# Dilated window attention and a gated MLP: plain q and k of six batches come through the crossbar, in the layout of the direct batches

## The chip, the cores and the metric

The kernel runs on one core of a Trainium2 chip. The metric is the device time of one execution in microseconds (us). Three executions of the kernel before took 310.85, 311.17 and 311.59 us; their median, 311.17, is the time before. The profile was taken from an execution of its own, with a span of 309.7 us.

## The reference

Attention over 8 batches, 8 heads, 576 tokens, 64 channels. Heads 0 to 3 ("plain") see the last 32 tokens, heads 4 to 7 ("dilated") every fourth of the last 128. An MLP with a swish gate follows.

```python
scores = scale * np.matmul(q, k.transpose(0, 1, 3, 2))
rel = pos[:, None] - pos[None, :]
mask_plain = (rel >= 0) & (rel < window)                                         # window 32, heads 0-3
mask_dil = (rel >= 0) & (rel < window * dilation) & (rel % dilation == 0)         # dilation 4, heads 4-7
attn = softmax(np.where(masks, scores, -1e9))
attn_out = np.matmul(attn, v)
x = attn_out.transpose(0, 2, 1, 3).reshape(B * S, H * D)      # 4608 tokens x 512
h = x @ w_in                                                   # 512 x 2048
g = h * (1.0 / (1.0 + np.exp(-beta * h)))
return g @ w_out                                               # 2048 x 512
```

Inputs and output are fp32; the kernel computes in bf16 with fp32 sums.

## The kernel before

A plan is made while the program is built: operations with their inputs, a rank `vt` and expected durations. A list scheduler puts them on the engines and gives out the eight PSUM banks. The order on every engine is then fixed; at run time each instruction waits only for its data. While TensorE is expected to wait early in the kernel, matmuls on zeros ("filler") are put in.

The MLP goes through 9 tiles of 512 tokens. For each, 16 blocks of `w_in` (four matmuls of 512 columns each), a tanh on ScalarE and a gate on VectorE, and later 4 blocks of `w_out` (16 matmuls each). Attention runs batch by batch beside it and leaves its output transposed in `xT`, in four parts of 128 channels: parts 0 and 1 are plain heads, 2 and 3 dilated. In the first tile four blocks are cut at token 288:

```python
    def slot_h(t, fb, c0, n, vt, xdeps):
        g = Group("h")
        def mms(e):
            for kt in range(NKT):                                    # the four parts of xT
                nc.tensor.matmul(bank(g)[:, 0:n], lhsT=w_in_bf[:, kt, fb * P:(fb + 1) * P],
                                 rhs=xT[:, kt, xo:xo + n], start=(kt == 0), stop=(kt == NKT - 1))
        ...  # tanh on ScalarE, gate on VectorE
        split = SPLIT if t == 0 else 0                               # SPLIT = 4
        order = [(fb, 0, S // 2) for fb in range(split)] + [(fb, S // 2, NTOK - S // 2) for fb in range(split)] + [
            (fb, 0, NTOK) for fb in range(split, NFB)]
```

q and k come in two ways. Batches 0 to 2 (`DIRECT = 3`) are loaded with tokens on partitions, cast to bf16 on the way, and transposed by TensorE. From batch 3 on, q and k are cast into a contiguous bf16 copy in DRAM, and a DMA transpose (crossbar) brings them into SBUF with channels on partitions:

```python
    def cast(b, z, deps, vt):
        dst = scratch[b, z] = dram_pool.tile([2, S * 4 * D], BF16, name=f"s{b}_{z}")
        src = (k, q)[z][b].rearrange("(x h) s d -> x (h s d)", x=2)
        return load("POOL", (dst[:].rearrange("x (a e) -> (x a) e", e=1024), src.rearrange("x (a e) -> (x a) e", e=1024)), ...)

    def crossbar(b, z, h0, deps, vt):
        flat = scratch[b, z][h0 // 4]
        if h0:                                                       # dilated heads
            dst = (dk, dq)[z][b % 2][:].rearrange("p r h t -> p r (h t)")
            src = flat.rearrange("(a e) -> a e", e=C * D)
        else:                                                        # plain heads: even and odd tokens in two halves of the partitions
            dst = raw[:, z].rearrange("p h m -> p (h m)").unsqueeze(1)
            src = flat.rearrange("(a e) -> a e", e=P)
        return plan.op([("SP", 1300)], lambda e: nc.sync.dma_start_transpose(out=dst, in_=src), ...)
```

For the plain heads of these batches, even and odd tokens are then spread by copies: k into `kz`, whose other rows stay zero, q into `qd`. So there are two forms of plain score, one in halves of the array and one over all 128 rows:

```python
            for e_ in range(2):
                def spread(e, e_=e_):                                # k: 2 copies a batch; q: 4 more
                    rows = slice(64 * e_, 64 * e_ + 64)
                    dst = kz[rows, :, WIN:].rearrange("p h (m e) -> p h m e", e=2)[:, :, :, e_]
                    copy(e, dst, raw[rows, 0])
            ...
            if b < DIRECT:                                           # two heads, one in each half of the rows
                ...
                            nc.tensor.matmul(
                                bank(gs[h])[:, a * QT:(a + 1) * QT], lhsT=kT[x][rows, i * QT:i * QT + P],
                                rhs=qT[rows, x, i * QT:(i + 1) * QT], start=b >= ADDED, stop=b >= ADDED or a == 2)
                continue
            g = Group("s")
            ...                                                      # all 128 rows, one head after another
                        nc.tensor.matmul(
                            sc[:, a, h2 * QT:h2 * QT + QT],
                            lhsT=kz[:, 2 * x + h2, i * QT:i * QT + P],
                            rhs=qd[:, 2 * x + h2, :, i * QT // 2:(i + 1) * QT // 2], start=True, stop=True)
```

A score is followed by an exponential on ScalarE, a mask multiply on GpSimd or VectorE, six value matmuls and a normalisation. Dilated heads have a main part and a tail of the last 16 tokens of each of the four residues (`T`, `U`). Batches 0 and 1 go into `xT` by TensorE; from batch 2 on the rows are stored to DRAM (plain rows in two stores by parity from batch 3, the tail in four) and come back through the crossbar. The last block of the output is made of two halves, the second evacuated by two engines and stored by two queues.

Of the kernel before, what the change touches and what calls it, by code (L numbers as in the profile page):

```python
# [22 lines left out]
class Op:  # L23
    def __init__(self, engs, fn, deps, vt, acquire, group, dma, lat):
        self.engs, self.fn, self.vt, self.acquire = engs, fn, vt, acquire
        self.deps = [d for d in deps if d is not None]
        self.dma, self.lat, self.group = dma, lat, group
        self.end = self.ready = None
        self.waits = 0
        self.next = []  # L30
        for g in group if isinstance(group, list) else [] if group is None else [group]:
            g.users.append(self)


class Plan:
# [3 lines left out]
    CAPS = {"h": 3, "o": 2, "z": 4, "a": 8, "s": 5}  # L39
# [6 lines left out]
    def op(self, engs, fn, deps=(), vt=0.0, acquire=None, group=None, dma=0, lat=None):  # L46
        acquire = acquire if acquire is None or isinstance(acquire, list) else [acquire]
        o = Op(engs, fn, deps, vt, acquire, group or acquire, dma, lat)
        self.ops.append(o)
        return o  # L50

    def run(self, filler=None, filler_until=0.0):
# [13 lines left out]
        ends = []  # L66

# [19 lines left out]
        while n_left:  # L87
# [25 lines left out]
            if filler is not None and s <= filler_until and free["PE"] + 300 < s:  # L113
# [5 lines left out]
                free["PE"] = now + 225  # L119
                continue  # L120
# [6 lines left out]
            o.fn(e)  # L127
            free[e] = s + d
# [28 lines left out]
FIRST = "KD0 QD0 KD1 QD1 KP0 QP0 KP1 QP1 S2 S3 T S00 S10 V20 V21 V30 V31 U V00 V10 X2 X3 X00 X10 S01 S11 V01 V11 X01 X11"  # L157
LATER = "S2 S3 T V20 V21 V30 V31 U S00 S10 S01 S11 X2 X3 V00 V10 X00 X10 S02 S12 V01 V11 X01 X11"
# [3 lines left out]
def kernel(  # L162
# [34 lines left out]
    DIRECT = 3  # L197
    ADDED = 1
    BY_DMA = 2
    SPLIT = 4  # L200
# [16 lines left out]
    def copy(e, out, in_):  # L217
# [10 lines left out]
    mask_e = {n: const([P, 2, 2, 2, QT // 2], BF16, f"maske_{n}") for n in ("FP", "PP")}  # L228
# [14 lines left out]
    ptt = const([P, 2, 288], BF16, "ptt")  # L243
    ptt_own = ptt[0:2 * KTL][:, :, 0:256].rearrange(
        "p c (h s) -> p c h s", h=4)[:, :, :, 0:2 * UT]
# [9 lines left out]
    raw = const([P, 2, 4, S // 2], BF16, "raw")  # L255
    vd16 = raw[:].rearrange("p z h m -> p (z h m)")[:, 0:1024].rearrange("p (h T d) -> p h T d", h=4, T=C)
    vd16_of = [vd16] * DIRECT + [st[b % 2][:, 0:1024].rearrange(
        "p (h T d) -> p h T d", h=4, T=C) for b in range(DIRECT, B)]
    kT = [const([P, WIN + S], BF16, f"kT{x}") for x in range(2)]
    kz = const([P, 4, WIN + S], BF16, "kz")  # L260
    qd = const([P, 4, 2, S // 2], BF16, "qd")
    qT = qd[:].rearrange("p (x f) e m -> p x (f e m)", x=2)[:, :, 0:S]
# [27 lines left out]
    def t_fill1(e):  # L290
        for x in range(2):
            nc.vector.memset(kT[x][:, 0:WIN], 0.0)
# [61 lines left out]
    def t_late(e):  # L354
        band(mask_d[:], [[0, 4]], [(1, P)], 0, WIN - 1, 1.0, 0.0)
        for n in ("PP", "FP"):
            band(mask_e[n][:].rearrange("p a b e m -> p (a b) e m"), [[0, 4]], [(1, 2), (2, QT // 2)],
                 WIN, -1, 1.0, 0.0)
            band(mask_n[n][:].rearrange("p a b n -> p (a b) n"), [[0, 4]], [(1, QT)], WIN, -1, 1.0, 0.0)
        nc.gpsimd.memset(mask_e["FP"][0:WIN, 0], 0.0)  # L360
        nc.gpsimd.memset(mask_n["FP"][0:WIN, 0], 0.0)
        nc.gpsimd.memset(kz[:], 0.0)  # L362
    late_fill = plan.op([("POOL", 11500)], t_late, vt=-.3)


# [15 lines left out]
    def plain_v(b, p0, c0):  # L381
        return bass.AP(tensor=v.tensor, offset=v[b, 0].offset + (p0 - WIN) * D + c0 * QT * D,
                       ap=[[D, (P if not p0 else P - WIN) if not c0 else WIN], [QT * D, 4 * NI - c0], [1, D]])

    def direct_vp(b, deps, vt):
        if b:
            return [load("POOL", (vp[b % 2][:, :, 0:D], plain_v(b, 0, 0)), deps, vt, 768, .27, 1450,
                         1100 if b < DIRECT else 4000)]
        return [load("POOL", (vp[0][WIN:P, :, 0:D], plain_v(0, WIN, 0)), deps, vt, 576, .25),
                load("POOL", (vp[0][0:WIN, 1:, 0:D], plain_v(0, 0, 1)), deps, vt, 184, .25)]  # L390

    def direct_vd(b, deps, vt, tdeps=()):
        src = v[b, 4:8].rearrange("h (t T) d -> t h (T d)", T=C)[0:P]
        out = [load("POOL", (vd16_of[b].rearrange("p h T d -> p h (T d)"), src), deps, vt, 512, .35)]
        for c in range(2):
            src = bass.AP(tensor=v.tensor, offset=v[b, 4].offset + ((P - WIN) * C + c) * D,
                          ap=[[2 * D, 2 * KTL], [S * D, 4], [1, D]])
            out.append(load("POOL", (vt_[b % 2][:, c, :, 0:D], src), list(tdeps), vt + (.15 if b == 0 else .02 if b < DIRECT else 0) + .001 + .001 * c, 96, .2))
# [4 lines left out]
    def cast(b, z, deps, vt):  # L403
        dst = scratch[b, z] = dram_pool.tile([2, S * 4 * D], BF16, name=f"s{b}_{z}")
        src = (k, q)[z][b].rearrange("(x h) s d -> x (h s d)", x=2)
        return load("POOL", (dst[:].rearrange("x (a e) -> (x a) e", e=1024),
                             src.rearrange("x (a e) -> (x a) e", e=1024)), deps, vt, 1152, .38)

    def crossbar(b, z, h0, deps, vt):
        flat = scratch[b, z][h0 // 4]  # L410
        if h0:
            dst = (dk, dq)[z][b % 2][:].rearrange("p r h t -> p r (h t)")
            src = flat.rearrange("(a e) -> a e", e=C * D)
        else:
            dst = raw[:, z].rearrange("p h m -> p (h m)").unsqueeze(1)
            src = flat.rearrange("(a e) -> a e", e=P)
# [31 lines left out]
    xcopy = {}  # L448

    def back_dma(b, j, vt_of, vdone):  # L450

        rows = dram_pool.tile([S // 2, HD], BF16, name=f"x{b}_{j}")
        plain = rows[:, 0:HD // 2].rearrange("(i m e) c -> e m i c", e=2, m=QT // 2)
        out = []
        if b < DIRECT:
            out.append(plan.op(
                [("SP", 500)], lambda e: nc.sync.dma_start(
                    out=rows[:, 0:HD // 2].rearrange("(i m) c -> m i c", m=QT),
                    in_=xsp[j][:].rearrange("p a x h d -> p a (x h d)")),
                [vdone[0, j], vdone[1, j]], vt_of[f"X1{j}"], dma=1200, lat=2000))  # L460
        for e_ in range(2 if b >= DIRECT else 0):
            out.append(plan.op(
                [("SP", 500)], lambda e, e_=e_: nc.sync.dma_start(
                    out=plain[e_], in_=xsp[j][e_ * QT // 2:(e_ + 1) * QT // 2].rearrange("p a x h d -> p a (x h d)")),
                [vdone[0, j], vdone[1, j]], vt_of[f"X1{j}"], dma=600, lat=2000))
# [7 lines left out]
        if j:  # L473
            for c in range(C):
                dil.append(plan.op(
                    [("SP", 500)], lambda e, c=c: nc.sync.dma_start(
                        out=right[t1 - t0:, c], in_=xdt[(c % 2 * 2 + c // 2) * UT:(c % 2 * 2 + c // 2 + 1) * UT].rearrange("p x h d -> p (x h d)")),
                    [vdone["U"]], vt_of["X11"], dma=150, lat=2000))
# [13 lines left out]
        for x in range(4):  # L492
            xcopy[b, x, j] = o

    def attention(b, ld, names, vts):
# [4 lines left out]
        if b < DIRECT:  # L500
            for n in [x for x in names if x[0] in "KQ"]:
# [8 lines left out]
                def evac(e, g=g, z=z, kind=kind, i=i):  # L510
                    tp = bank(g, BF16)[:, 0:S]
                    if kind == "P":
                        dst = qT[:, i] if z else kT[i][:, WIN:]
# [4 lines left out]
                key = (("kT", "qT")[z], i) if kind == "P" else (("dk", "dq")[z], kv, i)  # L518
                steps[n] = [plan.op([dve(S), act(S)], evac, [tr, fill1] + war(key), vt, group=g)]
                wrote(key)  # L520
        else:
            vt = vt_of["zPRE"]
            ready = {"D": [ld["x", 0, 4], ld["x", 1, 4]]}
            ops = []
            for e_ in range(2):
                def spread(e, e_=e_):
                    rows = slice(64 * e_, 64 * e_ + 64)
                    dst = kz[rows, :, WIN:].rearrange("p h (m e) -> p h m e", e=2)[:, :, :, e_]
                    copy(e, dst, raw[rows, 0])
                o = plan.op([("POOL", 1200), ("DVE", 1400)], spread, [ld["x", 0, 0], late_fill] + war("kz"), vt)  # L530
                used(("raw", 0), o)
                ops.append(o)
            wrote("kz")
# [468 lines left out]
```

The softmax here doesn't subtract the row's maximum and nothing guards it: scores larger than these inputs give would overflow.

## Time and profile before

| what | value |
|---|---|
| time, median of three | 311.17 us |
| span of the profiled execution | 309.7 us |
| granted TensorE clock | 0.998 |
| matmuls of w_in and w_out, 512 columns | 576 and 571 recorded |
| plain scores over all rows | 120, of 96 columns |
| transposes of q and k on TensorE | 72 of 96 columns, 216 of 64 |
| DMA, software queue (casts, loads) | 19.66 MB, 42336 packets |
| DMA, hardware queue (crossbars, stores) | 22.37 MB, 51052 packets |

In the profile PE is TensorE, DVE is VectorE, ACT is ScalarE, POOL is GpSimd and SP is SyncE. A line of a timeline gives the start and length of a run of equal instructions in us, the engine, the line of the kernel, what is written from what, and, in brackets, how long the engine stood idle before and what it waited for. TensorE overlaps its matmuls, so the difference of two starts tells what one costs, and not its own length. A line of the list of DMA issues ends with the size and the median time from issue to landing.

### The profile page before, as it was taken

The page shows a single profiled execution, that of the slowest core. Times are in us where ns is not written, and L with a number is a line of the kernel's source. Part 1 is how long each engine was busy: PE and PEld are TensorE (multiplying, and loading weights), DVE is VectorE, ACT ScalarE, POOL GpSimd, SP SyncE. Part 2 cuts the span into 40 slices and gives each one's busy share as a digit, 9 for nine tenths or more (in the row PEclk, how much of TensorE's full clock was granted, in tenths as well). Part 3 has the DMA queues.
Part 4 walks back from the last instruction along what each step waited for, and adds up shares of the span by engine and source line. Part 5 has one row for each costly group of instructions (what it writes and reads, how often), then busy time and mean ns, then how long its engine had stood idle before and what let it go on. Part 6 is the DMA issues. An engine that isn't in the chain of part 4 may idle for free.

```text
span 309.7 us, 6029 instructions
## 1 busy us (share of the span) xinstructions
PE 297.0 (96%) x2270; PEld 153.6 (50%) x2307; DVE 199.1 (64%) x421; ACT 171.3 (55%) x302; POOL 108.6 (35%) x150
## 2 busy tenths in 40 slices
PE   7899999999999999999999999999999999999994
PEld 5565546454454445444455454445544444444452
DVE  4687868888958777775896878677853443434300
ACT  2668845866448445753775547555754544554311
POOL 8989754537170146414823651154000000000000
PEclk9999999999999999999999999999999999999999
DMA  6999999999689982999999759997024100001112
GB/s 100 168 210 207 206 187 208 230 155 174 155 163 178 191 151 83 180 160 181 188 206 181 197 117 177 129 224 163 18 64 112 44 34 34 36 34 60 42 70 69
DMA packets 93561, 42.48 MB, mean 137 GB/s; under 512 B 71052, under 2 KB 88220, under 8 KB 93212
## 3 DMA queue, kind: packets, MB, share of 16 engines
q0 software_dynamic: 42336, 19.66, 50.3%
q1 hardware_dynamic: 51052, 22.37, 35.0%
q8 instruction: 18, 0.29, 0.4%
q14 instruction: 11, 0.09, 0.1%
q10 hardware_dynamic: 144, 0.07, 0.1%
HBM read 39.32 MB, written 18.87 MB: 188 GB/s over the span
## 4 chain that ended last, share of the span: by engine, by line
PE 82%; POOL 6%; DMA 6%; DVE 2%; issue 2%; ACT 0%; POOLq 0%; ACTq 0%; DVEq 0%
PE bank L856 38%; PE bank L824 35%; DMA raw<-in_v_dram 3%; DMA vp<-in_v_dram 3%; PE bank L703 2%; PE bank L755 2%; POOL st L368 1%; PE bank L740 1%; PE bank L644 1%; PE bank L725 1%; POOL kz L362 1%; DVE qt L218 1%; DVE g L836 1%; PE bank L434 0%; PE bank L618 0%
## 5 line engine op out<-in xcount | busy, mean ns | idle before, releaser
L831 ACT ACTIVATE tnh<-bank,beta_half 128x512 bf16<-128x512 f32 (+2 forms) x148 | 100.1, 677 | 81.8 <-PE bank L824 73.6
L836 DVE SCALAR_TENSOR_TENSOR g<-tnh,bank 128x512 bf16<-128x512 bf16 (+2 forms) x148 | 98.7, 670 | 69.2 <-ACT tnh L831 68.1
L824 PE MATMUL bank<-xT,w_in_bf 128*128 128x512 bf16 (+2 forms) x576 | 139.8, 373 | 1.3 <-DVE xT L218 0.3
L856 PE MATMUL bank<-w_out_bf,g 128*128 128x512 bf16 (+1 forms) x571 | 137.7, 373 | 1.8 <-DVE g L836 0.5
L856 PEld LDWEIGHTS <-g 128*128 128x128 bf16 x592 | 55.4, 98 | 58.6 <-issue 0.8
L824 PEld LDWEIGHTS <-w_in_bf 128*128 128x128 bf16 x592 | 55.1, 98 | 58.2 <-issue 0.8
L873 ACT ACTIVATE osb<-bank 128x512 f32<-128x512 f32 (+2 forms) x36 | 21.0, 582 | 28.4 <-PE bank L856 23.5
L586 ACT ACTIVATE pt<-bank 128x384 bf16<-128x384 f32 (+1 forms) x54 | 22.0, 455 | 6.4 <-PE bank L703 3.5
L586 ACT ACTIVATE ptd<-bank 128x512 bf16<-128x512 f32 x32 | 17.0, 601 | 10.3 <-PE bank L644 10.3
L605 DVE TENSOR_TENSOR xsp<-bank,rcp 96x384 bf16<-96x384 f32 x32 | 17.7, 554 | 1.1
L604 DVE RECIPROCAL rcp<-bank 128x4 f32<-128x4 f32 (+2 forms) x72 | 12.8, 177 | 5.5 <-PE bank L755 2.8
L218 POOL COPY kz<-raw 64x1152 bf16<-64x1152 bf16 x6 | 9.4, 1566 | 18.4 <-DMA raw<-s 18.3
L218 POOL COPY vd<-st 128x1024 bf16<-128x1024 bf16 x4 | 4.1, 1037 | 30.9 <-DMA st<-in_v_dram 30.9
L590 DVE TENSOR_TENSOR ptd<-ptd,mask_d 128x512 bf16<-128x512 bf16 x24 | 13.0, 575 | 2.8 <-ACT ptd L586 2.5
L605 DVE TENSOR_TENSOR xdm<-bank,rcp 128x256 bf16<-128x256 f32 x32 | 13.6, 424 | 1.1
L590 POOL TENSOR_TENSOR pt<-pt,maske_FP 128x384 bf16<-128x384 bf16 x7 | 6.3, 912 | 20.4 <-ACT pt L586 12.4
L368 POOL DMA_DIRECT2D vp<-in_v_dram x9 | 12.0, 1338 | 2.6 <-DMA vp<-in_v_dram 2.6
L755 PEld LDWEIGHTS <-pt 128*128 128x128 bf16 x192 | 9.2, 97 | 6.5 <-DVE pt L590 0.6
L755 PE MATMUL bank<-vp,pt 128*128 128x65 bf16 x192 | 10.6, 193 | 0.9 <-DVE pt L590 0.5
L368 POOL DMA_DIRECT2D vt<-in_v_dram x16 | 11.0, 694 | 0.0
L875 DVE TENSOR_SCALAR osb<-bank 128x512 f32<-128x512 f32 (+1 forms) x2 | 1.0, 486 | 13.7 <-ACT osb L873 13.7
L218 DVE COPY qd<-raw 64x1152 bf16<-64x1152 bf16 x14 | 8.9, 634 | 0.9 <-DMA raw<-s 0.8
(125 smaller groups left out, 223.4 us busy)
## 6 DMA issues: line engine op xcount, KB each, us to landing
out_dram<-osb SPq DMA_DIRECT2D x35, 256.0 KB, 2.0
s<-in_k_dram POOLq DMA_DIRECT2D x5, 576.0 KB, 7.6
s<-in_q_dram POOLq DMA_DIRECT2D x5, 576.0 KB, 10.2
vp<-in_v_dram POOLq DMA_DIRECT2D x7, 384.0 KB, 14.8
w_out_bf<-in_moe_w_out_dram POOLq DMA_DIRECT2D x2, 1024.0 KB, 16.3
st<-in_k_dram POOLq DMA_DIRECT2D x6, 288.0 KB, 13.3
st<-in_q_dram POOLq DMA_DIRECT2D x6, 288.0 KB, 13.5
x<-xsp SPq DMA_DIRECT2D x20, 72.0 KB, 2.3
```

The source lines that it names most:

```text
L218: (nc.scalar.copy if e == "ACT" else E[e].tensor_copy)(out=out, in_=in_)
L368: {"POOL": nc.gpsimd, "SP": nc.sync}[queue].dma_start(out=out, in_=in_)
L586: nc.scalar.activation(out=w(), in_=sc(), func=ACT.Exp, scale=SCALE)
L590: E[e].tensor_tensor(out=w(), in0=w(), in1=m(), op=ALU.mult)
L604: nc.vector.reciprocal(out=r, in_=p[..., D])
L605: nc.vector.tensor_tensor(out=dst, in0=p[..., 0:D], in1=r.unsqueeze(len(p.shape) - 1).to_broadcast(list(p.shape[:-1]) + [D]), op=ALU.mult)
L755: nc.tensor.matmul(pv[:, a, h2, :], lhsT=pt[x][:, (3 * j + a) * 2 + h2], rhs=vp[kv][:, (2 * x + h2) * NI + 3 * j + a, 0:D + 1], start=True ...
L824: nc.tensor.matmul(bank(g)[:, 0:n], lhsT=w_in_bf[:, kt, fb * P:(fb + 1) * P], rhs=xT[:, kt, xo:xo + n], start=(kt == 0), stop=(kt == NKT - 1))
L831: nc.scalar.activation(out=th[:, 0:n], in_=bank(g)[:, 0:n], func=ACT.Tanh, scale=beta_half[:, fb:fb + 1])
L836: nc.vector.scalar_tensor_tensor(out=g_t[t % 2][:, fb, c0:c0 + n], in0=th[:, 0:n], scalar=1.0, in1=bank(g)[:, 0:n], op0=ALU.add, op1=ALU.mult)
L856: nc.tensor.matmul(bank(g)[:, lo:hi], lhsT=g_t[t % 2][:, fb, tb * P:(tb + 1) * P], rhs=w_out_bf[:, fb, lo:hi], start=(fb == 0), stop=(fb = ...
L873: nc.scalar.mul(out=ob[:, cols], in_=bank(g)[:, cols], mul=0.5)
```

## The change

Its purpose is one layout of plain q and k for all batches. The plain heads are cast into token rows (all four heads of a token side by side), so that the crossbar brings them straight into the layout of the direct batches, now double-buffered. `raw`, `kz`, `qd` and the copies into them go, and so does the second form of score. Only batches 0 and 1 stay direct. Stores of attention rows become fewer: plain rows in one store, the tail in one. In the first tile, four blocks of `w_in` are computed apart: the sum over the dilated parts of `xT` first, the plain ones later in the same bank. The tail of batches 0 and 1 gets its own transposes (`Y2`, `Y3`) and can come later. The v load of batch 0 comes in three pieces by head, its tail load is ranked later, masks are made one by one, and the scheduler is told of a cost of 95 ns for a change between half and full rows. The last output block is made in pieces of 256, 128 and 128 columns.

```diff
-    CAPS = {"h": 3, "o": 2, "z": 4, "a": 8, "s": 5}
+    CAPS = {"h": 3, "p": 4, "o": 2, "z": 4, "a": 8, "s": 5}
+    SWITCH = 95
...
-LATER = "S2 S3 T V20 V21 V30 V31 U S00 S10 S01 S11 X2 X3 V00 V10 X00 X10 S02 S12 V01 V11 X01 X11"
+LATER = "S2 S3 T V20 V21 V30 V31 U S00 S10 X2 X3 V00 V10 X00 X10 S01 S11 V01 V11 X01 X11"
...
-    DIRECT = 3
+    DIRECT = 2
...
-    SPLIT = 4
+    APART = 4
...
-    raw = const([P, 2, 4, S // 2], BF16, "raw")
-    kT = [const([P, WIN + S], BF16, f"kT{x}") for x in range(2)]
-    kz = const([P, 4, WIN + S], BF16, "kz")
-    qd = const([P, 4, 2, S // 2], BF16, "qd")
+    kT = [const([P, 2, WIN + S], BF16, f"kT{i}") for i in range(2)]
+    qT = [const([P, 2, S], BF16, f"qT{i}") for i in range(2)]
...
-        return [load("POOL", (vp[0][WIN:P, :, 0:D], plain_v(0, WIN, 0)), deps, vt, 576, .25),
-                load("POOL", (vp[0][0:WIN, 1:, 0:D], plain_v(0, 0, 1)), deps, vt, 184, .25)]
+        half = 2 * NI
+        return [load("POOL", (vp[0][WIN:P, 0:half, 0:D], plain_v(0, WIN, 0)[:, 0:half]), deps, vt, 288, .25),
+                load("POOL", (vp[0][0:WIN, 1:half, 0:D], plain_v(0, 0, 1)[:, 0:half - 1]), deps, vt, 92, .25),
+                load("POOL", (vp[0][:, half:, 0:D], plain_v(0, 0, half)), deps, vt, 384, .27)]
...
+    def cast(b, z, h0, deps, vt):
+        dst = scratch[b, z, h0] = dram_pool.tile([S * 4 * D], BF16, name=f"s{b}_{z}_{h0}")
+        src = (k, q)[z][b, h0:h0 + 4]
+        if h0:
+            args = (dst[:].rearrange("(a e) -> a e", e=1024), src.rearrange("h s d -> (h s d)").rearrange("(a e) -> a e", e=1024))
+        else:
+            args = (dst[:].rearrange("(s h d) -> h s d", h=4, d=D), src)
+        return load("POOL", args, deps, vt, 576, .38 if h0 else .25)
...
-            dst = raw[:, z].rearrange("p h m -> p (h m)").unsqueeze(1)
-            src = flat.rearrange("(a e) -> a e", e=P)
+            dst = qT[kv][:] if z else kT[kv][:, :, WIN:]
+        src = scratch[b, z, h0][:].rearrange("(a e) -> a e", e=C * D)
...
-            for c in range(C):
-                dil.append(plan.op([("SP", 500)], ...   # four stores of the tail
+            dil.append(plan.op([("SP", 500)], ...       # one
...
-                    copy(e, dst, raw[rows, 0])          # and the copies of q; the whole branch goes
+            ready = {"D": [ld["x", 0, 4], ld["x", 1, 4]], "P": [ld["x", 0, 0], ld["x", 1, 0], fill1]}
...
+                        nc.tensor.matmul(
+                            bank(gs[h])[:, a * QT:(a + 1) * QT], lhsT=kT[kv][rows, x, i * QT:i * QT + P],
+                            rhs=qT[kv][rows, x, i * QT:(i + 1) * QT], start=b >= ADDED, stop=b >= ADDED or a == 2)
...
+        g = Group("p" if apart else "h")
+        parts = [((2, 3), 0, n), ((0, 1), 0, S // 2), ((0, 1), S // 2, n)] if apart else [((0, 1, 2, 3), 0, n)]
+        for i, (kts, a, z) in enumerate(parts):
...
-        for lo, hi in ((0, HD // 2), (HD // 2, HD)) if last_one else ((0, HD),):
+        cuts = (0, HD // 2, 3 * HD // 4, HD) if last_one else (0, HD)
```

## The prediction

> **What bounds the kernel now.** First the page: the share of each engine and the slices of TensorE, then its chain of work.
>
> ```profile
> span 309.7 us, 6029 instructions
> PE 297.0 (96%) x2270; PEld 153.6 (50%) x2307; DVE 199.1 (64%) x421; ACT 171.3 (55%) x302; POOL 108.6 (35%) x150
> ...
> PE   7899999999999999999999999999999999999994
> ...
> PE 82%; POOL 6%; DMA 6%; DVE 2%; issue 2%; ACT 0%; POOLq 0%; ACTq 0%; DVEq 0%
> ```
>
> TensorE is the bound, outside the first and the last slice. GpSimd, from which the change takes most, is busy for 35%. A busy TensorE hides what a matmul costs, since the records overlap; so I read starts, in the timeline of TensorE around 173 us:
>
> ```profile
> 172.75 1.89 PE L856 MATMUL bank<-w_out_bf,g 128*128 128x512 bf16 x8
> 174.57 0.63 PE L644 MATMUL bank<-dq,dk 64*128 64x128 bf16 x16
> 175.14 1.04 PE L856 MATMUL bank<-w_out_bf,g 128*128 128x512 bf16 x4
> ...
> 180.58 0.85 PE L703 MATMUL bank<-qd,kz 128*128 128x96 bf16 x16
> 181.27 1.89 PE L856 MATMUL bank<-w_out_bf,g 128*128 128x512 bf16 x8
> ```
>
> The old plain score (L703) takes (181.27 - 180.58)/16 = 43 ns a matmul. The eight L856 before the half-row scores take 1.82 us: 8 x 216 = 1.73 and 0.09 more, which appears wherever the tile mode of the array changes. In half-row mode two matmuls run as a pair; the second starts 4 ns after the first (median in the records).
>
> With 216 ns for 512 columns (other widths in proportion), one width per pair in half-array modes, and 95 ns for each of 73 mode changes, the instruction order adds up to 292.4 us. The last matmul ends near 305.3, so TensorE stands still for 12.9 us. Start by start, 8.0 of these are gone by 26 us, 9.7 by 42, 10.5 by 78; all the rest of the kernel has 2.4. The final 4.4 us are evacuation and store.
>
> The head, next:
>
> ```profile
> 15.70 0.20 PE L755 MATMUL bank<-vp,pt 128*128 128x65 bf16 x1
> 16.32 0.31 PE L755 MATMUL bank<-vp,pt 128*128 128x65 bf16 x5 [0.41 <-DMA vp<-in_v_dram]
> ...
> 20.07 1.14 PE L824 MATMUL bank<-xT,w_in_bf 128*128 128x288 bf16 x8 [0.27 <-DVE xT L218]
> ```
>
> ```profile
> 8.40 1.35 POOL L368 DMA_DIRECT2D vt<-in_v_dram  x2
> ...
> 11.55 0.76 POOL L368 DMA_DIRECT2D w_in_bf<-in_moe_w_in_dram  x1
> ```
>
> Values wait for v; the MLP starts at 20.07, when all four parts of xT of batch 0 are there. The first w_in piece landed 7.5 us after its issue (shortest landing in the answer on this tile), at 19.0.
>
> **What the Trainium skill says.** TensorE: Matmul & The Clock Gate, "Wait — 56ns, not 53.3ns?": warm matmuls follow each other at N/2.4 GHz + 2.5 ns; the 216 and 43 ns agree. TensorEngine Tiling (Array Packing), "Key Properties": a change of tiling mode drains the array; the trace agrees, at about 0.09 us a change. DMA: Bandwidth & Descriptors, "Why a DMA increments its semaphore by 16 and not by 1": a DMA is spread over the largest number of engines, up to 16, that divides the slowest dimension of both sides. The plain cast writes 4 heads x 576 tokens x 64, reading 2304 rows: that would be 4 engines. No transfer before has such a shape, so the trace is silent. Same page, "Specifications": under 512 B a transfer isn't at line rate; the new cast writes 128 B runs.
>
> **Part by part, in TensorE time.**
>
> (a) Batch 2 no longer transposes q and k on TensorE. By batch 1 in the timeline of TensorE: the 24 dilated ones come 12 at a time, 0.52 us each (28.35 to 28.87), 1.04; the 72 plain ones 36 at a time, 0.68 us each (31.25 to 31.93), 1.36. With the switches into that mode about 2.5 us, of which 2.1 is streaming.
>
> (b) Scores of batches 3 to 7. Removed: 120 x 43 ns = 5.1 us. Added: 120 half-row matmuls, 60 pairs x 42.5 = 2.55 us. But a full-array block now stands between small half-row groups: the changed order has 102 mode changes for 73, although batch 2's transposes took theirs away. 29 x 95 ns = 2.75 us. So the better-packed score gives back more than it wins.
>
> (c) Three waiting matmuls on zeros fewer: 0.33 us. Partial first sums have as many columns as the split ones they replace. The last block in pieces of 256, 128 and 128 has the same columns too; the last evacuation and store stay 128 columns wide.
>
> Sum: streaming -4.9, switches +2.75: 290.2 us for 292.4, **-2.2 us**.
>
> (d) Head. GpSimd issues the tail loads (1.35 us at 8.40) behind w_in, and one more load of v (about 0.4), so w_in is issued some 0.9 us earlier and, with 2 x 96 KB less ahead in its queue, lands near 18.1. Partial sums need only the dilated half of xT, and tail scores, tail values and their transposes now stand between MLP blocks. In TensorE's own work the MLP starts after 11.6 us instead of 12.7. Vd arrives no earlier, so I put the start at 18.3 to 18.6 instead of 20.07: the standstill before it is 6.8 instead of 7.4. Batch 1's loads come only some 0.6 us earlier and take part of that back. **-0.8 us.**
>
> (e) Off the path. The kz and qd copies go: on GpSimd 9.4 + 7.2 us, on VectorE 8.9 and some. ScalarE gets 40 exponentials of 288 columns more and loses 30 of 384 (0.455 us): about +1 us on an engine at 55%. VectorE masks twice as many, smaller blocks. None of this sets the end; it smooths waits such as the 0.7 us near 82 us (qt behind copies) and 0.7 near 104 (mask). **-0.5 us.** The stores of attention rows to DRAM become 28 fewer, and four crossbars are added; SyncE issues both and waits for casts and tiles anyway.
>
> Without a new wait: 311.2 (the time before; 1.5 above the profiled span) - 2.2 - 0.8 - 0.5 = 307.7.
>
> **Rivals.**
>
> *First: the plain cast becomes the wait.* Before, k and q came by contiguous casts:
>
> ```profile
> s<-in_k_dram POOLq DMA_DIRECT2D x5, 576.0 KB, 7.6
> s<-in_q_dram POOLq DMA_DIRECT2D x5, 576.0 KB, 10.2
> vp<-in_v_dram POOLq DMA_DIRECT2D x7, 384.0 KB, 14.8
> ```
>
> The new one has 2304 rows of 64. On 16 engines that is 144 packets each. In the records the 128-byte packets of this queue take 32 ns on average, and vp of batch 1 landed 2.6 us behind the load ahead, 192 packets an engine, 13 ns each. So 1.9 to 4.6 us, hidden. On 4 engines, 576 packets each: 7.5 to 18 us, and what follows in the rings of those engines waits too. Batches 4 to 7 have 20 us or more between GpSimd's issue and the plain score. Batches 2 and 3 haven't: their casts would be issued near 47 and 62 us, behind the weight loads (DMA is most loaded between 40 and 60), and their scores stand in the order at about 70 and 85. At 7.5 us it fits; at 18, batch 3's crossbars land near 90, and SyncE issues the return transposes of batch 2 only behind them, for which the third MLP tile waits at about 92. That would be 3 to 8 us: 311 to 316. The issue order and the shape speak for it; against it, that the scores stand late and that TensorE has other blocks to fill in.
>
> *Second: the switches are dearer, or the half-row scores hold two banks each and make matmuls wait for evacuation.* ScalarE and VectorE have room, so at most 1 to 2 us: 309.
>
> *Third: the waits on GpSimd's copies were worth more.* If the 4.9 us of standstill after 26 us mostly vanish, 304 to 305. The waits are small and have many releasers, with the loads among them, so this is less likely.
>
> **Range and chances.** I give 60% to the first sum, near 307.5, 30% to a stall of 2 to 6 us, the rest to both ends. Centre 308.2, range 305.2 to 313.5. Faster by 2% means under 304.95, which needs 3 us more than I can find: 0.10. Slower by 2% means over 317.4, a cast stall at the dear end: 0.08. Within 2%: 0.82.
>
> **What would show it.** Right: half-row scores whose block costs about 0.13 us and two changes of 0.09; no zero padding copies; first w_in matmul at 18.3 to 18.6; standstill under 12 us in total. Rival one: the landing time of the plain casts, over 10 us where the contiguous ones take less, and TensorE, at 70 to 95 us, ending a wait on kT, qT or xT. Wrong: w_in matmuls starting no earlier than 19.5, or standstill after 100 us above 3 us.

## The result, and the profile after

The changed kernel took 395.14 us (median of four, 394.19 to 395.41), the kernel before on the same chip 311.38 (four, 310.85 to 311.94). The ratio is 1.268, with a 95% interval of 1.265 to 1.272: 84 us slower, where 308.2 was predicted. Below, "before" and "after" are these two kernels.

The page of after, in the views that the prediction showed of before: engines, slices of TensorE and of its granted clock, packets, queue 0 (casts and loads), chain of work.

```profile
span 392.5 us, 5850 instructions
...
PE 308.6 (79%) x2216; PEld 150.7 (38%) x2216; DVE 184.8 (47%) x407; ACT 169.3 (43%) x310; POOL 114.1 (29%) x137
...
PE   7999798001999986100899969996699999999996
...
PEclk9999899555899998655699987999699999999999
...
DMA packets 207519, 43.96 MB, mean 112 GB/s; under 512 B 186036, under 2 KB 202308, under 8 KB 207300
...
q0 software_dynamic: 152080, 19.99, 68.1%
...
PE 45%; issue 25%; POOL 12%; DMA 10%; DVE 4%; ACT 2%; SPq 0%; POOLq 0%; DVEq 0%
```

Two holes of about 30 us stand in the slices of TensorE, and smaller ones elsewhere; in both the granted clock falls to half, too. The chain has 25% of "issue", time in which an engine waits for nothing that the profile shows; before had 2%. The bytes are nearly the same, but the packets have more than doubled (93,561 before), nearly all of it in the software queue (42,336 before). The lists of DMA issues and of waits say more:

```profile
s<-in_k_dram POOLq DMA_DIRECT2D x12, 288.0 KB, 16.5
s<-in_q_dram POOLq DMA_DIRECT2D x12, 288.0 KB, 12.8
```

```profile
POOL s L375 <- issue: 100.6, 8, 19.3
...
PE bank L600 <- POOL qt L226: 29.4, 1, 29.4
...
PE bank L683 <- POOL ptt L571: 29.3, 1, 29.3
```

The columns of the waits are the sum in us, how often, and the longest. GpSimd stands for 100.6 us in front of the issue of a cast. In its timeline around the first hole:

```profile
57.56 2.99 POOL L375 DMA_DIRECT2D s<-in_q_dram  x1 [10.62 <-issue]
...
75.21 3.01 POOL L375 DMA_DIRECT2D s<-in_k_dram  x1 [11.22 <-issue]
...
93.55 2.99 POOL L375 DMA_DIRECT2D s<-in_q_dram  x1 [13.20 <-issue]
96.54 0.30 POOL L226 COPY qt<-dq 64x128 bf16<-64x128 bf16 x1
```

The cast issued at 57.56 landed at 74.84, and the next could be issued at 75.21; that one landed at 93.17, and the next was issued at 93.55. All eight waits end like this, 0.4 us after the landing of the plain cast before. Behind this cast stands a copy of 0.30 us for which TensorE waits:

```profile
66.84 0.62 PE L626 MATMUL bank<-dq,dk 64*128 64x128 bf16 x16
96.89 0.45 PE L600 MATMUL bank<-qt,dkt 128*96 128x64 bf16 x4 [29.43 <-POOL qt L226]
```

With the costs of the prediction the order of TensorE's instructions still adds up to 290.2 us; its standstill rose from 12.9 to 98.7 us, while evacuation and store behind the last matmul fell from 4.4 to 3.6. The whole loss is standstill.

### The profile page after: what moved, and what is told of

It is laid out like the page before. It is cut to its first block, busy times and chain, and to the rows that moved or that the text cites. A ratio compares the mean times of both kernels' runs of the same rounds, so it can differ in the third digit from the quotient of the medians.

```text
span 392.5 us, 5850 instructions
## 1 busy us (share of the span) xinstructions
PE 308.6 (79%) x2216; PEld 150.7 (38%) x2216; DVE 184.8 (47%) x407; ACT 169.3 (43%) x310; POOL 114.1 (29%) x137
## 4 chain that ended last, share of the span: by engine, by line
PE 45%; issue 25%; POOL 12%; DMA 10%; DVE 4%; ACT 2%; SPq 0%; POOLq 0%; DVEq 0%
PE bank L830 23%; PE bank L795 18%; POOL s L375 7%; DMA vp<-in_v_dram 5%; DMA dk<-s 3%; DVE g L809 2%; POOL vt L375 2%; DMA st<-in_q_dram 1%; POOL vp L375 1%; DMA xT<-x 1%; POOL st L375 1%; PE bank L659 1%; PE bank L713 1%; POOL vd L226 1%; ACT ptd L567 1%
## 5 line engine op out<-in xcount | busy, mean ns | idle before, releaser
L804 ACT ACTIVATE tnh<-bank,beta_half 128x512 bf16<-128x512 f32 x144 | 98.2, 688 | 124.6 <-PE bank L795 123.4
L830 PE MATMUL bank<-w_out_bf,g 128*128 128x512 bf16 (+2 forms) x608 | 149.3, 378 | 0.0
L795 PE MATMUL bank<-xT,w_in_bf 128*128 128x512 bf16 (+1 forms) x584 | 146.4, 385 | 1.9 <-DVE g L809 1.5
L809 DVE SCALAR_TENSOR_TENSOR g<-tnh,bank 128x512 bf16<-128x512 bf16 x144 | 97.7, 685 | 83.9 <-ACT tnh L804 83.5
L375 POOL DMA_DIRECT2D s<-in_q_dram x12 | 21.0, 1749 | 83.6 <-issue 82.9
L845 ACT ACTIVATE osb<-bank 128x512 f32<-128x512 f32 (+1 forms) x35 | 20.6, 588 | 35.6 <-PE bank L830 34.7
L375 POOL DMA_DIRECT2D s<-in_k_dram x12 | 21.4, 1785 | 21.6 <-issue 17.7
L567 ACT ACTIVATE pt<-bank 128x288 bf16<-128x288 f32 x64 | 22.6, 412 | 10.5 <-PE bank L659 9.9
L683 PE MATMUL bank<-vt,ptt 96*64 96x65 bf16 x64 | 3.7, 204 | 29.3 <-POOL ptt L571 29.3
L571 POOL TENSOR_TENSOR ptt<-ptt,mask_t 96x256 bf16<-96x256 bf16 x5 | 3.4, 675 | 43.4 <-ACT ptt L567 43.3
## 6 DMA issues: line engine op xcount, KB each, us to landing
w_out_bf<-in_moe_w_out_dram POOLq DMA_DIRECT2D x2, 1024.0 KB, 16.3
```

Of the source, the lines that this page charges most:

```text
L375: {"POOL": nc.gpsimd, "SP": nc.sync}[queue].dma_start(out=out, in_=in_)
L567: nc.scalar.activation(out=w(), in_=sc(), func=ACT.Exp, scale=SCALE)
L683: nc.tensor.matmul(pv[:, h4], lhsT=ptt_of(c, h4), rhs=vt_[kv][:, c, h4, 0:D + 1], start=(c == 0), stop=(c == 1))
L795: nc.tensor.matmul(bank(g)[:, a:z], lhsT=w_in_bf[:, kt, fb * P:(fb + 1) * P], rhs=xT[:, kt, xo + a:xo + z], start=(i == 0 and kt == kts[0] ...
L804: nc.scalar.activation(out=th[:, 0:n], in_=bank(g)[:, 0:n], func=ACT.Tanh, scale=beta_half[:, fb:fb + 1])
L809: nc.vector.scalar_tensor_tensor(out=g_t[t % 2][:, fb, c0:c0 + n], in0=th[:, 0:n], scalar=1.0, in1=bank(g)[:, 0:n], op0=ALU.add, op1=ALU.mult)
```

## The experiments

Three theories stood against each other. *Issue:* the plain cast, with heads outermost, occupies its queue so long that GpSimd can't issue what follows. *Transfers:* it is the DMA traffic, by its packets or its moment, that makes the crossbars late. *Rest:* something else in the change (scores, banks, head) costs time. "TensorE's work" is always the sum over the instruction order with the prediction's costs; "standstill" is what the trace has beyond it up to the end of the last matmul; behind that come 3.3 to 4.5 us. Medians of before, run beside each group on the same chip, lie between 311.49 and 312.34.

**1 (e1). The same cast with tokens outermost.** The same rows of 64 values are moved; the order of instructions on all engines stays.

```diff
-            args = (dst[:].rearrange("(s h d) -> h s d", h=4, d=D), src)
+            args = (dst[:].rearrange("(s h d) -> s h d", h=4, d=D), src.rearrange("h s d -> s h d"))
```

> The changed kernel, with one edit: the plain cast walks tokens first and heads second, so that its slowest dimensions are 2304 and 576 in place of 4 and 2304. Bytes, 128-byte runs and the order on every engine stay the same. Shape theory (with 4 heads outermost the cast's data go over 4 DMA engines, the other 12 get small fillers, the next such cast can't be issued until the last has landed, and GpSimd stands still with all that queues behind it): software packets fall from 152,080 to about 41,500, one issue takes about 1.2 us in place of 3.0, no wait of over 3 us before a plain cast, time 305 to 310. Short-run theory (128-byte writes to DRAM are slow in themselves): the casts still take over 10 us to land, time over 360. Order theory (the new order on the engines waits by itself, whatever the cast): time over 380.

341.12 us, ratio 1.092 (1.086 to 1.099): 54 of the 84 us are gone with one line, though the expected 305 to 310 is missed. No cast waits any more without a releaser in the profile (one waits 5.1 us, and a load of v 12.5 us, for the landing of an earlier load). The packets of the software queue have halved, to 69,136 for the 41,500 expected:

```profile
DMA packets 124576, 43.63 MB, mean 129 GB/s; under 512 B 103093, under 2 KB 119365, under 8 KB 124357
...
q0 software_dynamic: 69136, 19.66, 63.8%
```

The difference, 82,944 packets, is 12 casts x 12 engines x 576, and all of them are 4 bytes long. So the cast of after had its 2304 rows on four engines, 576 each, and each of the other twelve got as many fillers of 4 bytes. The landing hardly changed: the twelve plain casts took 12.6 to 24.1 us from issue to landing in after (median 16.3), and 7.9 to 30.2 in e1 (median 15.4). What went with the 54 us is the wait in front of the issue, not the lateness of the data. Some 29 us remain.

**2 and 3 (e2, e3). The kernel before, with two additional plain casts a batch (3 to 7) that nobody reads,** heads outermost and tokens outermost.

```diff
+            for z in range(2):
+                extra = dram_pool.tile([S * 4 * D], BF16, name=f"extra{b}_{z}")
+                load("POOL", (extra[:].rearrange("(s h d) -> h s d", h=4, d=D), (k, q)[z][b, 0:4]), ...)
```

> The kernel before, with two extra plain casts for each of batches 3 to 7 in the heads-first shape of the change, into DRAM that nobody reads (10 extra casts, 5.9 MB read). Shape theory: each extra cast takes 3.0 us to issue and the second of each pair waits 10 to 18 us for the first to land; GpSimd still has the kz and qd copies to do in this kernel, so the time rises by 20 us or more. Order theory: the order is not that of the changed kernel, so the time rises by under 5 us.

387.79 us, ratio 1.237 (1.227 to 1.247), and the same wait:

```profile
POOL extra L368 <- issue: 109.9, 5, 27.3
```

> As the kernel before with two extra plain casts per batch, the same order on every engine, but the extra casts walk tokens first. Shape theory: each takes 1.2 us to issue, nothing waits for it, time 311 to 316. Short-run theory: as slow as the heads-first ones, within 3 us of that run.

One run of 321.05 us and three of 333.68 to 336.24, all above the 311 to 316 expected; the spread is too wide for a ratio. No cast waits for its issue. From issue to landing the two forms take equally long (shortest, median, longest; heads outermost first, then tokens outermost):

```profile
DMA to landing us min/median/max: 12.4/18.8/29.9
```

```profile
DMA to landing us min/median/max: 13.7/18.0/28.4
```

Both casts bring the same bytes into the same kernel, so 50 us and more hang on the order of the dimensions; and as nothing reads the result, lateness of the cast itself can't be the cause. But even the tokens-outermost form costs 9 us in its fastest run, and more in the others: the traffic matters.

**4 (e4). Each plain cast of after in two, of 288 tokens each,** heads outermost in both.

```diff
+            d3 = dst[:].rearrange("(s h d) -> h s d", h=4, d=D)
+            return [load("POOL", (d3[:, t0:t0 + S // 2], src[:, t0:t0 + S // 2]), deps, vt, 288, .25) for t0 in (0, S // 2)]
...
```

> The changed kernel with each plain cast in two casts of 288 tokens, still heads first. If the limit is room for descriptors (576 in each ring per cast, and a second 576 don't fit), the second half of 288 goes out while the first is in flight, waits before a cast are about half as long, and the time lies between, some 340 to 385. If only one such transfer can be under way, the second half waits for the first to land, and the time is that of the changed kernel, 390 or more, as there are more of them.

373.79 us, ratio 1.188 (1.179 to 1.197). GpSimd waits oftener and shorter, now before loads of v as well:

```profile
POOL s L375 <- issue: 44.6, 10, 8.9
...
POOL vp L375 <- issue: 24.0, 5, 8.8
```

Three halves (3 x 288 rows an engine) were issued before the first had landed; the fourth came at 54.07, after the first landed at 53.72. In after, two whole casts (2 x 576) never were under way together. So the limit isn't one cast at a time; it looks like room for the descriptors of an engine, between 864 and 1152 of them here. That is inferred from these moments, no record shows the room.

**5 (e17). Each plain cast in two, of two heads each** (one run).

```diff
+            d3 = dst[:].rearrange("(s h d) -> h s d", h=4, d=D)
+            return [load("POOL", (d3[i:i + 2], src[i:i + 2]), deps, vt, 288, .25) for i in (0, 2)]
```

> The changed kernel with each plain cast in two casts of 2 heads, heads first. Shape theory: 2 DMA engines carry the data of each (576 rows in each ring) and 14 get fillers, so software packets rise from 152,080 to about 262,000, each cast still takes 3.0 us to issue, and the waits before a cast are as long as in the changed kernel but twice as many: time well over 395, some 440 to 520. If the number of heads outermost doesn't matter: about 395.

537.15 us in the one run. A half cast now has two heads outermost. Its issue takes 3.0 us, as that of the whole one, and GpSimd waits twenty times, up to 18.4 us (the mean in the second line takes in six dilated casts of 0.5 us):

```profile
q0 software_dynamic: 262864, 20.44, 58.6%
...
L375 POOL DMA_DIRECT2D s<-in_k_dram x18 | 38.9, 2163 | 113.1 <-issue 109.2
```

The 4-byte packets of the 24 half casts are 24 x 14 x 576: two engines carry 576 rows each, fourteen get fillers. In these casts the outermost dimension sets the number of engines: 4 heads, 2 heads, or with tokens outermost all sixteen. The order of dimensions alone made 54 us; *Issue* stands for that part.

**6 to 9 (e5, e9, e6, e8). The size of the pieces of the dilated cast.** What remains is 29 us over before. In e1 the dilated cast (one row of 18 KB an engine) and the crossbars of the batch ahead are under way together. SyncE's instructions that issue crossbars, start and length, and TensorE's wait in the same stretch:

```profile
120.59 2.68 SPq L429 DMA_TRANSPOSE dq<-s  x1
123.36 15.31 SPq L429 DMA_TRANSPOSE kT<-s  x1
138.76 3.42 SPq L429 DMA_TRANSPOSE qT<-s  x1
...
141.73 1.04 PE L626 MATMUL bank<-dq,dk 64*128 64x128 bf16 x16 [11.84 <-DMA dq<-s]
```

The shortest of these instructions take 1.3 us (kT in after: 1.29 to 3.32). The length is that of SyncE's instruction and need not be the crossbar's own: TensorE's wait for dq ends only at 141.73. The packets started in 2 us, and their mean time:

```
us        256 B (crossbar)   128 B (casts, v)     18 KB (dilated cast)
122-124     826,  31 ns         820,  31 ns            none
130-132     185, 227 ns         178, 126 ns          4, 1966 ns
138-140     127, 248 ns         144, 131 ns          8, 1381 ns
142-144     516,  31 ns        1414,  32 ns            none
```

(The 128-byte packets are those of the plain casts and of the loads of v in the same queue.) While 18 KB packets are under way, the small ones come four to seven times more rarely in the stretches shown. The edit, on e1 (first with pieces of 2 KB, then, `e=256`, of 512 bytes), on after and on before:

```diff
-            args = (dst[:].rearrange("(a e) -> a e", e=1024), src.rearrange("h s d -> (h s d)").rearrange("(a e) -> a e", e=1024))
+            args = tuple(f.rearrange("(x a e) -> a x e", a=16, e=1024) for f in (dst[:], src.rearrange("h s d -> (h s d)")))
```

> The tokens-first kernel (341 us) with one edit more: the cast of the dilated heads goes in 144 pieces of 2 KB, nine a DMA engine, in place of one row of 18 KB an engine. Bytes and orders stay. Lockstep theory (in that run, 126 to 140 us, an 18 KB packet holds one engine for 1.4 us or more, the crossbar in flight waits for that engine, and the load behind it alternates with the crossbar packet for packet): the stretches with under 200 small packets a us go, crossbars on SyncE take under 6 us, time 305 to 318. Volume theory (too many 128-byte runs for the DMA engines beside the crossbars): the time stays within 4 us of 341. Batch-2 theory (the early loads are too many): no change either.

330.61 us, ratio 1.060 (1.055 to 1.065), for 1.092 of e1: between the expectations, so the 18 KB rows are a part of the 29 us and not the whole.

> The tokens-first kernel with the dilated cast in 576 pieces of 512 B, 36 a DMA engine (2 KB pieces gave 330.6 us, 18 KB rows 341). Lockstep theory (beside a crossbar all engines move at the pace of the one whose packet is longest): packets of 60 ns instead of 170 shorten the slow stretches again; under 325. If the slow stretches come from the pair of crossbar and v load by itself: 328 to 333, and stretches of under 400 small packets per 2 us remain between 60 and 74 and between 122 and 136 us.

324.49 us, 1.039 (1.034 to 1.044).

> The changed kernel, heads-first plain cast kept, with only the dilated cast in 2 KB pieces. If the two causes add up, the plain casts still wait for each other (some 100 us of issue waits on GpSimd) and the time falls by at most 30 us, to 360 to 390; if the 18 KB rows were the whole cause, it falls to under 320.

393.36 us, 1.260 (1.255 to 1.266), where up to 30 us less was expected: with heads outermost the pieces win 2 us at most. The waits in front of the plain casts stay at 97.6 us and probably cover the rest.

> The kernel before with its contiguous casts in 2 KB pieces. There the casts have landed before the crossbars start, so lockstep theory: within 2 us of the kernel before. If 18 KB rows are dear in themselves, it gets faster by 3 us or more.

311.50 us, 0.998 (0.995 to 1.001): where casts and crossbars don't meet, the size means nothing. The response to the size (1.092, 1.060, 1.039) supports *Transfers*; that one large packet holds up all engines is my reading of it, not shown by a record.

**10 (e10). Casts behind the crossbars of the batch before.** In the kernel before, a cast depends on all four crossbars of the batch ahead of its own; the change drops that dependency, in a line that the cut diff above leaves out and that the prediction passed over. Put back, on e1:

```diff
+            behind = [ld[b - 1]["x", z, h0] for z in range(2) for h0 in (0, 4)] if b > DIRECT else []
...
-                c = cast(b, z, h0, gop[b - 2, 0], b - 2 + .01 * n)
+                c = cast(b, z, h0, gop[b - 2, 0] + behind, b - 2 + .01 * n)
```

> The tokens-first kernel, 18 KB rows, but the casts of a batch are ranked behind the dilated crossbars of the batch before, as in the kernel before the change. Overlap theory (loads queued behind v, running beside the crossbars of the batch before, make the slow stretches): the long v landings of 10 us and more go, time 312 to 325. Volume theory: 338 or more.

320.82 us, 1.028 (1.024 to 1.032), with pieces of 18 KB still. TensorE's work 289.5, standstill 26.0, of which some 10 come between 66 and 105 us (before: about 1), where batch 2 is at work.

**11 to 13 (e7, e11, e12). Batch 2 direct again** (`DIRECT = 3`): on e1, on e10, and on e10 with pieces of 512 bytes.

> The tokens-first kernel with batch 2 direct again (18 KB rows kept). Batch-2 theory: the standstill between 70 and 90 us and most of the rest goes, under 320. Lockstep theory: the stalls move with the casts, since those of a batch still meet the crossbars of the one before: 325 to 345.

321.20 us, 1.029 (1.024 to 1.035), between the two expectations; TensorE's work 293.1, standstill 22.3, with one wait of 5.5 us on xT.

> Tokens first, casts behind, batch 2 direct. TensorE's own work is 293.1 us here by the same count (292.4 before, 290.2 changed). If overlap and batch 2 were all that is left, standstill is as before and the time 308 to 314.

311.51 us, 1.002 (0.997 to 1.006): even with before.

```profile
span 309.5 us, 6005 instructions
...
PE 79%; DMA 11%; DVE 4%; ACT 2%; issue 2%; SPq 1%; DVEq 0%; POOLq 0%
```

TensorE's work is 293.1 us with 110 changes of mode, standstill 13.1: what before had.

> The last kernel with the dilated cast in 512 B pieces. If pieces matter only where casts run beside crossbars, within 3 us of it.

312.10 us, 1.003 (0.998 to 1.008): the size no longer matters once the casts stay behind and batch 2 is direct.

**14 (e13). e10 with pieces of 512 bytes,** batch 2 through the crossbar.

> Tokens first, casts behind the crossbars of the batch before, dilated cast in 512 B pieces, batch 2 through the crossbar as in the change. TensorE's own work is 289.5 us by the count. If the rest was the long rows beside crossbars: 308 to 313. If it is batch 2's transfers in the busy stretch: 317 to 321, with the standstill between 66 and 105 us.

Over 22 runs the median is 318.21 (311.88 to 322.42), against 311.81 before; the ratio, 1.009 (1.006 to 1.012), counts only the seven runs within 1.5% of the fastest, and over all 22 it would be 1.02. In the trace (a run of 314.86 us): work 289.5, standstill 19.8, of which 7.6 between 66 and 105 us. All runs together speak for the second expectation, the fastest lie between the two: the rest is mostly batch 2's transfers in the busiest stretch, but not shown to be wholly that.

**15 and 16 (e14, e15). Half-row scores ranked together,** to save changes of mode, with batch 2 direct (on e12) and not (on e13).

```diff
-LATER = "S2 S3 T V20 V21 V30 V31 U S00 S10 X2 X3 V00 V10 X00 X10 S01 S11 V01 V11 X01 X11"
+LATER = "S2 S3 S00 S10 S01 S11 T V20 V21 V30 V31 U X2 X3 V00 V10 X00 X10 V01 V11 X01 X11"
```

> Batch 2 direct, casts behind, 512 B pieces, and the half-row scores of a batch ranked next to each other, so that the order has 98 mode changes in place of 110. At 95 ns each TensorE's work falls from 293.1 to 291.9: about 1.1 us faster than the same kernel without it (312.1; 309.0 of span), if nothing else waits more.

315.24 us, 1.012 (1.008 to 1.016), a miss. Changes of mode fell from 110 to 98 and the work to 291.9, but the plain scores now come before their crossbar:

```profile
PE bank L659 <- DMA qT<-s: 3.7, 1, 3.7
```

> The first of these three with its scores ranked together. If the other stalls stay, as much faster than it as its count of TensorE's work says.

314.77 us, 1.011 (1.007 to 1.015): 87 changes of mode, 288.8 us of work, the least of all kernels, and 22.2 of standstill; no faster than those seven runs of e13, a miss as well.

**17 (e16). The head alone, in the kernel before:** the blocks apart, v in three pieces, the tail loads and tail work later. In this version the tail rows of batches 0 and 1 go to places of other residues; the amount of work is the same.

```diff
+    APART = 4
-    SPLIT = 4
...
-...load("POOL", (vt_[b % 2][:, c, :, 0:D], src), list(tdeps), vt + (.15 if b == 0 else ...
+...load("POOL", (vt_[b % 2][:, c, :, 0:D], src), list(tdeps), vt + (1.245 if b == 0 else ...
...                                      # v in three pieces, T and U behind X, own transposes Y2, Y3
```

> The kernel before with the head of the change alone: dilated parts of the first sums apart, tail of batches 0 and 1 transposed later, v of batch 0 in three pieces, tail loads behind w_in. Casts, crossbars, copies and both forms of score as before. TensorE's work is 292.6 us by the count (292.4 before). The prediction's term: the MLP starts at 18.3 to 18.6 us and 0.8 us of standstill go; so 0.3 to 1.0 us faster than before, 310.5 to 311.2. If later loads take it back: no difference.

312.74 us over ten runs, for 311.49: 1.0035 (1.002 to 1.005), slightly slower. Work 292.6; standstill 7.6 us by 26 us (before 8.0), but 11.2 by 42 us (before 9.7). One wait makes most of that difference:

```profile
40.24 1.04 PE L874 MATMUL bank<-w_out_bf,g 128*128 128x512 bf16 x4 [1.48 <-DMA w_out_bf<-in_moe_w_out_dram]
```

The first load of `w_out` is issued at 31.02 us here, behind all the masks on GpSimd, at 18.23 in before and at 20.95 in after, where the masks are made one by one. So this kernel loses by an order that the change doesn't have, and doesn't settle what the change's head is worth.

## Why the prediction was wrong, step by step

TensorE's own work and standstill before the tail, by the same account, beside the median:

| kernel | work | standstill | median us |
|---|---|---|---|
| before | 292.4 | 12.9 | 311.4 |
| after | 290.2 | 98.7 | 395.1 |
| e1, tokens outermost | 290.2 | 43.6 | 341.1 |
| e10, casts behind | 289.5 | 26.0 | 320.8 |
| e11, batch 2 direct too | 293.1 | 13.1 | 311.5 |

What comes behind the last matmul is not in these columns. It takes 4.0 to 4.5 us in every trace with the old last block and 3.3 to 3.6 in every one with the new. The prediction counted nothing for it in (c); it was not tried by itself, but it is what makes e11, with more work than before, even with it.

*The step that failed is rival one's:* "Batches 4 to 7 have 20 us or more between GpSimd's issue and the plain score", with "3 to 8 us: 311 to 316". The number for one cast, 7.5 to 18 us on 4 engines, was near. The Trainium skill's rule (DMA: Bandwidth & Descriptors, "Why a DMA increments its semaphore by 16 and not by 1"), which the prediction cited without a trace to hold it against, agrees with what the fillers now count: 4 engines for 4 heads, 2 for 2. The twelve casts took 12.6 to 24.1 us from issue to landing. The prediction treated those 18 us as a delay of what the cast brings, needed late and by two batches only. They are also an occupation of the issuer: the next plain cast isn't issued until this one has landed, and once GpSimd has come to it, it does nothing else meanwhile. Two casts a batch take 33 us in the mean, in a kernel with some 39 us a batch (309.7 / 8): the twelve are 198 us of transfers one after another, and GpSimd stood still in front of eight of them. The small copies and masks in its order (`qt`, `ptt`, `pt`) then come up to 30 us late, and TensorE waits for those, again and again. I had asked when the cast lands and who reads it, not what stands behind it on the engine that issues it. A busy share of 35% for GpSimd looked like room; in after the share is 29%, and GpSimd sets the pace. Nor was the landing time, which the prediction named as the sign of this rival, the sign: e1 has it nearly unchanged. e1, e2, e4 and e17 show it; taken back first, it is worth 54 of the 84 us. (With casts held back and batch 2 direct the form with heads outermost was not run; the shares might be others in that order.)

*A second step failed with it,* at the end of (e): "four crossbars are added; SyncE issues both and waits for casts and tiles anyway", and in rival one the cast on 16 engines, "1.9 to 4.6 us, hidden": in e1 the plain casts took 7.9 to 30.2 us on 16 engines. The change also drops the dependency that kept a batch's casts behind the crossbars of the batch ahead, and puts batch 2's casts and crossbars into the stretch where DMA is most loaded. With tokens outermost this costs 29 us; holding the casts back wins 20 of them, and batch 2 on TensorE the other 9. The two overlap, since either alone leaves 9 (e7, e10).

*(a) to (c), the sum of -2.2 us:* by the orders it stands, 290.2 for 292.4. A block of half-row scores, in the timeline of TensorE of after:

```profile
220.23 1.04 PE L795 MATMUL bank<-xT,w_in_bf 128*128 128x512 bf16 x4
221.20 0.30 PE L659 MATMUL bank<-qT,kT 64*128 64x96 bf16 x6
221.44 0.82 PE L830 MATMUL bank<-w_out_bf,g 128*128 128x512 bf16 x3
```

From 221.20 to 221.44 are 0.24 us: 0.13 for three pairs and one change of 0.11; the four matmuls ahead take 0.97, that is 0.86 and the other change. But the gain hangs on batch 2's transposes leaving TensorE, and that costs standstill (e10 for e11). With batch 2 direct the work is 293.1, 0.7 more than before: the new score form alone, as (b) said, gives back more than it wins.

*(d) The head, -0.8 us:* right as far as it looked, but no gain is left by 42 us. In after:

```profile
18.43 0.34 PE L713 MATMUL bank<-vp,pt 128*128 128x65 bf16 x6
18.61 1.02 PE L795 MATMUL bank<-xT,w_in_bf 128*128 128x512 bf16 x4
```

The MLP starts at 18.61 (18.3 to 18.6 predicted, 20.07 before), and by 26 us the standstill is 7.24 for 8.04, just 0.8 less. By 42 us it is 10.35 for 9.71, a difference smaller than that between traces with the same head (up to 1.3 us among before, e2, e3 and e8). The prediction let batch 1's loads take "part of that back"; in after the longest wait of TensorE between 26 and 42 us is another, for a copy of batch 1's v on VectorE:

```profile
41.29 0.78 PE L698 MATMUL bank<-vd,ptd 128*128 128x65 bf16 x16 [1.98 <-DVE vd L226]
```

Before, the same matmuls waited 0.26 us there, at 40.17. Whether another order of these copies would keep the 0.8 us stays open; e16, which waits for `w_out` instead, doesn't tell.

*(e), -0.5 us for the copies that go:* not found. e11 has none of the `kz` and `qd` copies, and its standstill is that of before. Rival three falls with it. Rival two: the changes of mode cost what was worked out; in after one half-row score waits 3.5 us for a gate on VectorE, in e11 none does.

The range failed because all its cases counted stalls of single transfers; none let a stall come back in each batch.

## What to carry to other kernels

Before a DMA's access pattern is changed, work out from the outermost dimensions on how many engines it will run, and put a dimension that 16 divides outermost (here 576 tokens in place of 4 heads); a rearrangement that moves the same rows was worth 54 us here. A long transfer costs its issuer too: look at what stands behind it in that engine's order, and who waits for that; the busy share of that engine doesn't show it, and neither does the landing time. And read a dropped dependency between transfers as part of the change: it may be what kept them apart.

## What the runs showed of the hardware

- A software-queue cast on k engines has as many 4-byte packets for each of the others as the k carry rows, by the counts: 6,912 for 2,304 rows at k = 4, 8,064 for 1,152 rows at k = 2. GpSimd spends 3.0 us on issuing either, 1.6 to 2.2 us with tokens outermost, 0.5 us on a contiguous 288 KB cast. The Trainium skill (DMA: Bandwidth & Descriptors, "Anatomy of one DMA — SWDGE (gpsimd) path") calls the generation of descriptors small, with many to be had before the cost shows. Here the cost shows, and in front of the next such cast a wait of up to 27.3 us (e2).
- 256-byte crossbar packets beside 18 KB cast packets took 227 ns for 31 ns in the mean (e1), and one of SyncE's instructions that issue a crossbar 15.31 us, where the shortest in after took 1.29.
- A standstill of 30 us lowers TensorE's granted clock, too: 0.53 in the stretch from 68 to 97 us, 0.90 over the whole of after. Right behind it four matmuls of 512 columns take 1.69 us (97.16 to 98.85), for 0.87 ahead of it (63.29 to 64.16).
